# The last head set of an attention block as two halves, the last MLP by token tile, and a shared PV bank

## The chip, the cores and the metric

The kernel runs on one core of a Trainium2 chip. The metric is the device time of one execution in microseconds (us). Engines are named as in the profile: PE is TensorE, ACT is ScalarE, DVE is VectorE, POOL is GpSimd, SP is SyncE, which issues most DMAs.

## The reference

A transformer block with conditioning (adaLN) over 2048 tokens of width 640, with 32 heads of width 20 and an MLP of width 1536 whose gate and up parts are multiplied without a nonlinearity:

```python
mod = (_silu(c) @ w_mod).reshape(1, 6, 1, -1)          # sa, ca, ga, sb, cb, gb
h = _layernorm(x) * (1 + ca) + sa
x = x + ga * attention(h, wqkv, wo)                    # softmax(q k^T / sqrt(20)) v, 32 heads, then wo
h = _layernorm(x) * (1 + cb) + sb
x = x + gb * (((h @ w_gate) * (h @ w_up)) @ w_down)
```

Inputs and output are bfloat16.

## The kernel before

The program is written by a planner that runs in the kernel's own Python. Every operation becomes a `Task` with an engine, a duration, dependencies, a priority, and buffer slots; `Sched.run` steps through planned time, and on each engine starts the ready task of lowest priority number. PE has its own chooser, `pick_pe`. `emit_program` then writes each engine's list in that order, with semaphore waits only where a dependency crosses engines. So one changed duration, slot or setting moves instructions all over the program.

**Attention.** The queries are cut into five chunks, `CHUNKS`: three of 512 tokens, two of 256. The heads go in 8 sets of 4. A chunk and a set are an *item* (40 items). An item consists of *units*: 512 columns of scores of one head (keys by queries), made on PE at L1480 from `QT` and `KT`, four heads in four row groups of 32. Two units fill two PSUM banks, and one exponential on ACT (L1517, `PP<-ps_all` 128x1024) turns them into probabilities. Some units go to DVE instead, four to a *quad*, as `QUADS` says by chunk and set: L1541 turns each score bank into an integer (task P1, tile `DB`), L1573 and L1581 make two terms of 2048 columns (`DSS`), and a product of the two is done by DVE in one piece (L1578) or by POOL in four (L1593). Quads count as two terms in the next step, so a unit on DVE costs PE two products where one on ACT costs one.

**PV.** At L2038 the probabilities are multiplied by `Vf` (V with a column of ones), four heads in four column groups, and summed over all keys of the item in one PSUM bank, number 7 (`BPV`). At an item's end a DVE transpose (L1665, T1) empties the bank; the next item's first PV product waits for it (`st_pv["free"]`). Then come a reciprocal (L1669), a product on POOL (L1671), a transpose back (L1679), and small DMAs on SP (L1692) that place the head outputs in `Ocp`.

**PSUM.** Banks 0, 1, 3 and 4 hold the scores for ACT. A pool `G` of banks 5, 6 and 2 serves P1 units and every other product; bank 7 is PV's.

**Other work on PE** fills the time between scores, in `Round`s that each take one bank of `G`, run a chain of products and end with an evacuation: the projections K, Q and V, and for each finished chunk the suffix (`suffix`): the output projection with residual (L1763), layer norm, transposes (L1796), gate and up (`gsb` takes the gate out of PSUM, L1865 or L1896 multiplies it into `hprod`), down, and the residual sum (L1919) that a DMA writes out (L1928). Most of these products use 32-column tiles (L939), the last chunk's full 128-column ones (L935). K and Q of head set 0 (and of some others) come straight out of PSUM; the rest is packed in blocks of 128 rows (L1199) and goes through DRAM (`k_rows`, `q_rows`) to be laid out by head. V is made per 128 tokens in the parts that `V_PARTS` lists:

```python
V_PARTS = [[0, 4], [4, 8]]
K_ALL = (0,)
LATEQ = (3,)
```

`K_ALL` names the 512-token chunks whose K is made directly for all sets, `LATEQ` those whose Q is made only in the second attention chunk. The suffix of chunk c runs between the scores of chunk c+1. The last chunk's has no scores beside it; its DMAs, with weights from `stx` and `stg`, are issued earlier. Its output projections need the last head set's result only in their last product (`wo7`, `OcT`), which is split off (`OP_EARLY`).

**Filler.** Two fillers keep PE active where it has nothing ready: `do_fill` (L2403, L2405) with products of the identity, and `zero_fill` (L2377), which adds products of a zero tile `zt` to the PV bank. `STAGE` holds the chooser's settings item by item (thresholds for PV bursts, for filling, for holding PE free for a score).

Of the kernel before, what the change touches and what calls it, by code (L numbers as in the profile page):

```python
# [12 lines left out]
SEM = 60.0  # L13
# [21 lines left out]
class Task:  # L35
    __slots__ = ("head", "hval", "hknow", "eng", "dur", "lat", "deps", "emits", "ctr", "prio", "gate", "acq", "on_start", "slots",
                 "start", "done", "needed", "val", "know", "nleft", "ready", "users", "name", "mode", "seq", "rt", "sem",
                 "nbytes", "cond", "alt", "land", "lk")

    def __init__(self, eng, dur, emits, deps=(), ctr=None, prio=0.0, lat=None, gate=0, acq=(), on_start=None,  # L40
# [26 lines left out]
        self.lk = 0  # L67
        if lat is None:
            lat = {"pe": PE_DRAIN, "act": ACT_LAT, "dve": DVE_LAT, "pool": 60.0}.get(eng, 0.0)
        self.lat = lat  # L70

# [49 lines left out]
class Sched:  # L121
# [32 lines left out]
    def locked(self, eng, task):  # L154
        if not task.lk:
            return False
        if self.lk_end["pool" if eng == "dve" else "dve"] > self.t:
            return True
        if task.lk == 2:
            tt = max(self.t, self.free_at["dve"])  # L160
            for d in sorted(self.readyl["dve"], key=lambda x: (x.prio, x.seq)):
# [89 lines left out]
    def pull(self, eng):  # L251
        p = self.pend[eng]
        while p and p[0][0] <= self.t:
            _, _, task = heapq.heappop(p)
            self.readyl[eng].append(task)

    def step_engine(self, eng):
# [4 lines left out]
        rl.sort(key=lambda x: (x.prio, x.seq))  # L262
        for k, task in enumerate(rl):
            if task.gate > self.progress or (task.cond is not None and not task.cond()):
# [13 lines left out]
    def steal(self):  # L278
# [4 lines left out]
        for task in self.readyl["dve"]:  # L283
            if task.alt is not None and (best is None or (task.prio, task.seq) < (best.prio, best.seq)):
                best = task
        if best is None or self.free_at["dve"] <= self.t and best is min(self.readyl["dve"], key=lambda x: (x.prio, x.seq)):
# [41 lines left out]
def emit_program(nc, sched, nsem_dma=56):  # L328
# [97 lines left out]
    with nc.Block() as block:  # L426
# [20 lines left out]
        def _(e):  # L447
# [5 lines left out]
QUADS = ((0, 4, 3, 3, 3, 4, 4, 4),  # L453
# [35 lines left out]
K_ALL = (0,)  # L489
# [6 lines left out]
V_PARTS = [[0, 4], [4, 8]]  # L496
# [14 lines left out]
FILL_Z, Z_LATE = 3300.0, 0.0  # L511
# [9 lines left out]
OPFIRST = 0  # L521
# [4 lines left out]
LATEQ = (3,)  # L526
LATEQ_A = 2
LATEQ_F = 0.534
# [4 lines left out]
    0: {"X_LATE": -179.96, "D_RES": 74, "EAGER": 9, "PVMAX": 14, "HOLD": 95, "PVTOL": 249, "D_LATE": 16, "PVMIN": 2, "PVCAP": 12, "FILL_MIN": 4190.746, "TPRIO": 0.75, "XDPRIO": 1.343, "XBACK": 0, "STEAL_GAP": 200, "FILL_Z": 3300.0, "Z_LATE": 0.0},  # L533
    1: {"HOLD": 91, "D_LATE": 10, "PVMAX": 7, "Z_LATE": 89.79, "FILL_MIN": 4705.4},
    2: {"DL": 0.376, "D_LATE": 17, "D_RES": 29, "FILL_Z": 3209.68, "EAGER": 9, "FILL_MIN": 4297.75},
    3: {"STEAL_GAP": 200, "PVMAX": 5, "FILL_MIN": 4667.05, "PVTOL": 199},
    4: {"XBACK": 0, "PVMAX": 9, "EAGER": 4},
    5: {"EAGER": 7, "D_RES": 27, "PVCAP": 8, "XBACK": 2, "FILL_MIN": 3800.69, "PVMIN": 5, "PVTOL": 124, "HOLD": 155},
    6: {"PVCAP": 12, "FILL_MIN": 4293.4, "D_LATE": 12, "PVMIN": 2, "EAGER": 8, "TPRIO": 0.87},
    7: {"DL": 0.501, "PVCAP": 8, "PVTOL": 347, "FILL_MIN": 4921.03, "D_LATE": 18, "HOLD": 155, "PVMAX": 9},  # L540
    8: {"PVCAP": 15, "PVMAX": 3, "FILL_MIN": 3871.81, "Z_LATE": -44.68, "FILL_Z": 3323.21},
    9: {"X_LATE": -14.35, "PVCAP": 14, "FILL_Z": 3486.74, "XBACK": 0, "HOLD": 80, "PVMIN": 5, "D_LATE": 12, "PVMAX": 5},
    10: {"PVMAX": 8, "X_LATE": -27.967, "EAGER": 8, "D_LATE": 15, "PVCAP": 14, "XBACK": 0, "HOLD": 155, "FILL_Z": 3693.44, "Z_LATE": -95.95},
    11: {"DL": 0.443, "X_LATE": 44.62, "FILL_MIN": 4364.854, "PVTOL": 245, "HOLD": 134, "PVMAX": 9, "PVCAP": 13},
    12: {"DL": 0.459, "FILL_MIN": 5309.94, "D_LATE": 7, "STEAL_GAP": 194.93, "X_LATE": -138.337},
    13: {"DL": 0.417, "D_RES": 4, "HOLD": 84, "PVMAX": 6, "TPRIO": 0.787, "PVMIN": 5, "STEAL_GAP": 145.61, "PVCAP": 13, "XBACK": 3, "FILL_MIN": 4476.6, "FILL_Z": 2814.04},
    14: {"D_LATE": 14, "D_RES": 22, "FILL_MIN": 4216.3, "EAGER": 10, "X_LATE": 83.38, "STEAL_GAP": 200, "PVTOL": 324, "FILL_Z": 3248.09},
    15: {"X_LATE": -197.47, "FILL_MIN": 4338.164, "EAGER": 13, "Z_LATE": -100, "D_RES": 5, "HOLD": 95, "PVCAP": 15},
    16: {"FILL_MIN": 4469.77, "D_RES": 61, "HOLD": 88, "PVCAP": 11, "PVMIN": 3, "PVTOL": 299, "STEAL_GAP": 121.93, "EAGER": 10},
    17: {"D_LATE": 17, "PVMAX": 10, "PVMIN": 5, "STEAL_GAP": 195.663, "FILL_MIN": 4059.54},  # L550
    18: {"FILL_MIN": 5006.36, "D_RES": 10, "X_LATE": 47.914, "FILL_Z": 3093.15, "HOLD": 65, "Z_LATE": -17.94, "PVTOL": 174},
    19: {"DL": 0.471, "D_LATE": 18, "FILL_MIN": 3976.707, "X_LATE": -139.98, "HOLD": 110},
    20: {"DL": 0.391, "D_LATE": 14, "PVCAP": 16, "FILL_MIN": 5166.07, "FILL_Z": 3745.27, "HOLD": 125, "STEAL_GAP": 143.97},
    21: {"D_RES": 10, "PVCAP": 20, "HOLD": 111, "PVMAX": 6, "PVMIN": 2, "D_LATE": 19, "X_LATE": -18.564, "STEAL_GAP": 193.54, "FILL_MIN": 4920.22},
    22: {"PVMAX": 6, "FILL_MIN": 3112.0, "D_RES": 17, "X_LATE": -139.27, "EAGER": 6, "D_LATE": 16, "PVCAP": 10, "FILL_Z": 2965.54, "PVTOL": 224},
    23: {"PVTOL": 197, "PVMAX": 8, "D_RES": 20, "Z_LATE": -56.49, "STEAL_GAP": 273.34, "FILL_MIN": 5000.65, "EAGER": 4, "HOLD": 170},
    24: {"DL": 0.464, "PVCAP": 13, "PVMAX": 9, "PVMIN": 2, "FILL_MIN": 3616.91, "EAGER": 7, "STEAL_GAP": 200, "X_LATE": 41.65, "HOLD": 125, "XDPRIO": 0.3, "D_LATE": 14},
    25: {"DL": 0.549, "STEAL_GAP": 200, "HOLD": 129, "X_LATE": 33.41, "D_RES": 10, "FILL_MIN": 3705.17, "PVCAP": 13, "D_LATE": 18, "PVMIN": 5, "Z_LATE": 116.92, "PVMAX": 9, "XBACK": 1},
    26: {"DL": 0.411, "D_RES": 15, "X_LATE": -208.68, "PVMAX": 9, "PVCAP": 14, "STEAL_GAP": 200, "FILL_MIN": 3859.63, "XBACK": 3, "EAGER": 8},
    27: {"DL": 0.473, "D_LATE": 6, "PVMAX": 6, "EAGER": 2, "D_RES": 75, "PVTOL": 249, "PVMIN": 2, "X_LATE": -47.659, "FILL_MIN": 4666.31},  # L560
    28: {"PVCAP": 13, "X_LATE": 63.33},
    29: {"PVCAP": 14, "PVMAX": 7, "D_RES": 46, "FILL_MIN": 3820.529, "HOLD": 65, "PVTOL": 299},
    30: {"X_LATE": -28.91, "PVCAP": 18, "FILL_MIN": 3782.61, "D_LATE": 16, "EAGER": 6, "PVMAX": 4, "STEAL_GAP": 217.05, "PVTOL": 224},
    31: {"D_RES": 19, "FILL_MIN": 4905.173, "D_LATE": 15, "PVMIN": 2, "X_LATE": 36.868, "HOLD": 125, "PVTOL": 274},
    32: {"PVMIN": 1, "D_LATE": 17, "D_RES": 78, "XDPRIO": 0.559, "XBACK": 0, "X_LATE": 56.51, "FILL_Z": 2800.13, "EAGER": 3},
    33: {"DL": 0.442, "STEAL_GAP": 199.702, "D_LATE": 18, "PVCAP": 15, "PVMAX": 4, "PVTOL": 353, "D_RES": 11, "PVMIN": 2, "HOLD": 100, "XDPRIO": 1.634, "EAGER": 4, "Z_LATE": 171.35, "FILL_MIN": 5185.17},
    34: {"X_LATE": 150, "D_LATE": 22, "HOLD": 117, "FILL_MIN": 3598.58, "EAGER": 5},
    35: {"PVMIN": 5, "PVMAX": 8, "FILL_MIN": 2725.18, "STEAL_GAP": 179.748, "X_LATE": -77.47, "HOLD": 121, "D_LATE": 8},
    36: {"DL": 0.524, "PVMIN": 2, "D_RES": 10, "X_LATE": -6.364, "FILL_MIN": 4268.89, "PVMAX": 8, "HOLD": 33},
    37: {"D_LATE": 12, "PVTOL": 179, "PVCAP": 13, "FILL_MIN": 5500, "X_LATE": -66.154, "TPRIO": 0.3, "XBACK": 0, "XDPRIO": 1.88, "HOLD": 65},  # L570
    38: {"D_RES": 60, "PVMAX": 7, "PVTOL": 450, "HOLD": 67, "D_LATE": 16},
    39: {"FILL_MIN": 3000, "D_LATE": 13, "PVTOL": 258, "X_LATE": -31.59, "PVCAP": 16, "PVMAX": 5, "EAGER": 8, "HOLD": 140, "XBACK": 3},
# [15 lines left out]
def build_kernel(nc, A_x, A_wqkv, A_wo, B_x, B_w_gate, B_w_up, B_w_down, c, w_mod, out):  # L588
# [62 lines left out]
    zt = alloc("zt", [128, 32], BF16)  # L651
# [33 lines left out]
    Vf = alloc("Vf", [128, NT * H * VW], BF16)  # L685
# [56 lines left out]
    set_r = (hprod, h2T, xck, xn2)  # L742
    ntail = CHUNKS[-2][1]
# [20 lines left out]
    G = Slots([5, 6, 2] if HEADG else [5, 6], "G")  # L764
# [3 lines left out]
    BPV = 7  # L768
# [113 lines left out]
    p_zt = pool(100, lambda e: e.memset(zt[:], 0.0), prio=5) if FILL_Z > 0.0 else None  # L882
# [1598 lines left out]
```

## Time and profile before

| | us |
|---|---|
| median of 3 runs | 811.79 |
| the runs | 813.02, 810.24, 811.79 |
| profiled execution: span from first to last instruction | 809.0 |
| PE busy | 792.6 |
| ACT busy | 763.8 |
| DVE busy | 703.1 |
| POOL busy | 321.2 |

The profiled execution has no other time than its span; the median lies 2.8 us above it. A busy share is an average over a start, in which projections feed the first scores, a long middle, and an end without scores, so the stages have to be read one by one. The granted clock of PE is 1.00. In a timeline, a row gives the start, how long the merged group lasts, the engine, the line, the operation, how many, and in brackets the idle time before it with what ended it. In a windows row the columns are the window, its length, the busy time and number of instructions, the granted clock, the DMA share and GB/s.

### The profile page before, as it was taken

What the parts mean: (1) busy time and instruction counts of PE and PEld (TensorE: products, weight loads), DVE (VectorE), ACT (ScalarE), POOL (GpSimd) and SP (SyncE); (2) the same over time, 40 slices, a digit from 0 to 9 for tenths busy, and PEclk for the clock granted to TensorE, in tenths of its full rate; (3) what the DMA queues carried; (4) which work ended last, traced back from release to release, by engine and by line L of the source; (5) the groups of instructions that cost most, each with busy time, mean ns of one, the idle gap of its engine ahead of it and who ended that gap; (6) DMA issues with size and microseconds to landing.
All of it is one profiled execution on the core that took longest, in us unless ns stands there. A gap on an engine that the chain in (4) does not pass through costs nothing.

```text
span 809.0 us, 29314 instructions
## 1 busy us (share of the span) xinstructions
PE 792.6 (98%) x12585; PEld 303.1 (37%) x12585; DVE 703.1 (87%) x1273; ACT 763.8 (94%) x853; POOL 321.2 (40%) x330
## 2 busy tenths in 40 slices
PE   9999999999999999999999999999999999999998
PEld 4433333222232333233233232343244433444567
DVE  7979987999999999999998999999699875778973
ACT  7899999999999999999999999999999999999912
POOL 3304244565524442164335334444265340443520
PEclk9999999999999999999999999999999999999999
DMA  9633211113330144100301221001201236005520
GB/s 306 210 87 105 71 46 42 47 36 123 91 67 25 40 112 132 26 9 20 85 25 31 48 57 30 11 22 53 56 6 31 55 78 144 23 30 125 115 70 17
DMA packets 116447, 54.74 MB, mean 68 GB/s; under 512 B 83915, under 2 KB 116319, under 8 KB 116319
## 3 DMA queue, kind: packets, MB, share of 16 engines
q1 hardware_dynamic: 115391, 51.72, 24.3%
q8 instruction: 100, 1.64, 0.8%
q10 hardware_dynamic: 928, 1.15, 0.4%
q14 instruction: 28, 0.23, 0.1%
HBM read 41.85 MB, written 8.41 MB: 62 GB/s over the span
## 4 chain that ended last, share of the span: by engine, by line
PE 52%; ACT 34%; DVE 8%; issue 4%; SPq 1%; DMA 0%; POOL 0%; ACTq 0%; POOLq 0%
ACT PP L1517 34%; PE ps_all L1480 17%; PE ps_all L939 15%; PE ps_all L2038 11%; DVE DB L1541 3%; PE ps_all L935 3%; PE ps_all L1199 3%; PE ps_all L1135 1%; PE ps_all L2403 1%; DVE DSS L1581 1%; DVE DSS L1578 1%; PE ps_all L2405 1%; DVE DSS L1573 1%; PE ps_all L1096 1%; DVE wd L1463 0%
## 5 line engine op out<-in xcount | busy, mean ns | idle before, releaser
L1517 ACT ACTIVATE PP<-ps_all 128x1024 bf16<-128x1024 f32 x808 | 743.9, 1144 | 5.2 <-PE ps_all L1480 4.4
L1593 POOL TENSOR_TENSOR DSS<-DB,DSS 128x512 bf16<-128x512 bf16 x224 | 254.9, 1156 | 324.6 <-DVE DSS L1581 236.0
L1541 DVE TENSOR_SCALAR DB<-ps_all 128x512 int16<-128x512 f32 x432 | 288.5, 684 | 45.0 <-PE ps_all L1480 42.2
L1480 PE MATMUL ps_all<-QT,KT 32*128 32x512 bf16 (+1 forms) x2560 | 315.7, 340 | 8.3 <-ACT PP L1517 5.9
L1480 PEld LDWEIGHTS ps_all<-QT,KT 32*128 32x128 bf16 x2560 | 82.4, 91 | 266.3 <-ACT PP L1517 230.0
L2038 PE MATMUL ps_all<-PP,Vf 128*32 128x512 bf16 (+1 forms) x2032 | 158.8, 343 | 0.3 <-DVE OT L1665 0.3
L939 PE MATMUL ps_all<-h2T,stg 128*32 128x512 bf16 (+1 forms) x1744 | 118.1, 345 | 1.2 <-DVE DB L1541 0.9
L2038 PE MATMUL ps_all<-DSS,Vf 128*32 128x512 bf16 (+2 forms) x1056 | 84.4, 343 | 0.4 <-POOL DSS L1593 0.2
L1573 DVE TENSOR_SCALAR DSS<-DB 128x2048 int16<-128x2048 int16 x108 | 75.5, 699 | 0.5
L1581 DVE TENSOR_SCALAR DSS<-DB 128x2048 int16<-128x2048 int16 x108 | 75.8, 702 | 0.0
L2038 PEld LDWEIGHTS ps_all<-PP,Vf 128*32 128x32 bf16 x2032 | 44.6, 94 | 78.4 <-issue 72.1
L1671 POOL TENSOR_TENSOR OTn<-OT,invT 128x512 bf16<-128x512 f32 (+1 forms) x39 | 37.8, 970 | 89.4 <-DVE invT L1669 89.3
L1578 DVE TENSOR_TENSOR DSS<-DB,DSS 128x2048 bf16<-128x2048 bf16 x52 | 67.1, 1290 | 0.2
L939 PE MATMUL ps_all<-wd,hprod 128*32 128x320 bf16 (+1 forms) x1348 | 60.1, 282 | 0.0
L939 PEld LDWEIGHTS ps_all<-h2T,stg 128*32 128x32 bf16 x1744 | 37.2, 95 | 35.7 <-issue 23.6
L939 PEld LDWEIGHTS ps_all<-wd,hprod 128*32 128x32 bf16 x1348 | 29.7, 96 | 19.7 <-issue 11.3
L2038 PEld LDWEIGHTS ps_all<-DSS,Vf 128*32 128x32 bf16 (+1 forms) x1056 | 26.4, 95 | 19.7 <-issue 8.2
L939 PE MATMUL ps_all<-wV,hT 128*32 128x320 bf16 (+1 forms) x692 | 31.7, 291 | 0.0
L1885 DVE CAST gsb<-ps_all 128x512 bf16<-128x512 f32 x36 | 24.5, 680 | 8.1 <-PE ps_all L939 8.0
L1199 PE MATMUL ps_all<-hT,wq 128*32 128x512 bf16 x375 | 31.5, 382 | 0.0
L1665 DVE STREAM_TRANSPOSE OT<-ps_all 128x512 f32<-128x512 f32 (+1 forms) x40 | 24.1, 603 | 7.3 <-PE ps_all L2038 7.3
L939 PE MATMUL ps_all<-wo,Ocp 128*32 128x320 bf16 (+1 forms) x648 | 29.8, 283 | 0.6 <-DVE DB L1541 0.2
(124 smaller groups left out, 531.6 us busy)
## 6 DMA issues: line engine op xcount, KB each, us to landing
stg<-in_B_w_gate_dram SPq DMA_DIRECT2D x50, 160.0 KB
stg<-in_B_w_up_dram SPq DMA_DIRECT2D x50, 160.0 KB
QT<-q_rows SPq DMA_DIRECT2D x22, 128.0 KB
KT<-k_rows SPq DMA_DIRECT2D x84, 32.0 KB
wm<-in_w_mod_dram SPq DMA_DIRECT2D x3, 800.0 KB
x<-in_A_x_dram SPq DMA_DIRECT2D x7, 320.0 KB
xck<-in_A_x_dram SPq DMA_DIRECT2D x3, 640.0 KB
wd<-in_B_w_down_dram SPq DMA_DIRECT2D x1, 1920.0 KB
```

Of the source, the lines that this page charges most:

```text
L939: return lambda e, b: e.matmul(ps[32 * x:32 * x + 32, b, c0 + o:c0 + o + w], lhs()[:, 32 * x:32 * x + 32], rhs() if w == n else rhs()[:, o ...
L1199: f = [lambda e, b_, k=k, x=x: e.matmul(ps[x:x + min(32, w - x), b_, :], wx[:, k, r0 + x:r0 + min(x + 32, w)], hT[tc][:, k, :], tile_posit ...
L1480: ems.append(lambda e, i=i, kt=kt: e.matmul(dstf()[:, i * u.n:(i + 1) * u.n], KT[32 * u.s:32 * u.s + 32, u.j, kt * 128:(kt + 1) * 128], QT ...
L1517: return e.activation(PPs[g % 2][:, cellp["p"], 0:nu * 512], ps[:, b0:b0 + nu, :].rearrange("p b c -> p (b c)"), AFT.Exp, scale=ESCALE)
L1541: return e.tensor_scalar(DBl[st_["slot"]][:, x * 512:(x + 1) * 512], bank(cell["b"]), EBIAS, 0.0, op0=ALU.add, op1=ALU.max)
L1573: return e.tensor_scalar(DSl[st_["ss"][0]][:, :], DBl[st_["slot"]][:, :], 0x7F, 0x3F00, op0=ALU.bitwise_and, op1=ALU.bitwise_or)
L1578: return e.tensor_tensor(d, DBl[st_["slot"]][:, :].bitcast(BF16), d, ALU.mult)
L1581: return e.tensor_scalar(DSl[st_["ss"][1]][:, :], DBl[st_["slot"]][:, :], 0x7F80, 2, op0=ALU.bitwise_and, op1=ALU.bitwise_or)
L1593: return e.tensor_tensor(d, DBl[st_["slot"]][:, x * w:x * w + w].bitcast(BF16), d, ALU.mult)
L1671: f3 = lambda e: e.tensor_tensor(OTn[:, 0:n].rearrange("p (b c r) -> p b r c", c=32, r=2), OT[:, 0:n].rearrange("p (b r c) -> p b r c", c= ...
L1885: f = lambda e: e.tensor_copy(gsb[:, gs, 0:n], ps[:, r.b["b"], 0:n])
L2038: ems.append(lambda e, i=i, kt=kt, stt=stt, stp=stp: e.matmul(ps[32 * s:32 * s + mc, BPV, 0:u.n], Vf[:, (kt * H + 4 * u.j + s) * VW:(kt * ...
```

## The change

- The last item (chunk 4, set 7) becomes two items of 128 queries each (`SPLITJ`, `spans`), without quads (`QHALF`), where the whole item had two. A unit still has 512 score columns, now four key tiles by 128 queries.
- The suffix of the last chunk is done per tile of 128 tokens: transposes and their evacuation per tile (`t_h2t`), gate and up in rounds of two 128-wide blocks of the MLP for one tile (`hp_t`), output projections per tile as soon as that tile's head outputs are there; only the second tile's last products are split off.
- PV takes a bank from `G`, which has now 5, 6, 2 and 7, at an item's first product, and gives it back at T1. Two items may be open at once (`PV_OPEN`), the second one only if two banks are free (`PV_KEEP`). `zero_fill` goes.
- V is made in four parts, K of chunk 0 is packed for all sets but the first, and the Q of a second 512-token chunk is made late.
- Chunk 1 has a residual buffer of its own, `xckb`, in the place of dead queries.
- Output projections of every chunk get an earlier priority (`OPFIRST`), the settings in `STAGE` are others, and a few changes make the planner itself run faster (sorted ready lists, `dead` tasks).

```diff
-V_PARTS = [[0, 4], [4, 8]]
+V_PARTS = [[0, 2], [2, 4], [4, 6], [6, 8]]
-K_ALL = (0,)
+K_ALL = ()
-OPFIRST = 0
+OPFIRST = 1500
-LATEQ = (3,)
-LATEQ_A = 2
-LATEQ_F = 0.534
+LATEQ = (2, 3)
+LATEQ_A = -20
+LATEQ_F = 0.35
+SPLITJ = 1
+QHALF = ((0, 0), (0, 0))
+PV_W4 = 430.0
+PV_OPEN = 2
+PV_KEEP = 2
...
-    G = Slots([5, 6, 2] if HEADG else [5, 6], "G")
+    G = Slots([5, 6, 2, 7], "G")
-    BPV = 7
...
+    if SPLITJ:
+        del items[-SPLITJ:], spans[-SPLITJ:], nqs[-SPLITJ:]
+        for hf in range(2):
+            for x in range(SPLITJ):
+                items.append((NC - 1, NSET - SPLITJ + x))
+                spans.append((128 * hf, 128))
+                nqs.append(QHALF[hf][x])
...
+    xckb = at("xckb", [128, 4, D], BF16, qt_off)
+        if ci % 2 and not alt:
+            xck = xckb
+            xfree = outs_r[1] + sfx_done["qd0"] + x0_done
...
         def one(u, srcf, deps, name):
+            info = item_info[u.item]
+            if info["bank"] is None:
+                info["bank"], rel = G.take(G.avail()[1], 1)
+                deps = deps + rel
...
+            for tl in range(ntl):
+                for f2 in range(0, FT, 2):
+                    mms = []
+                    for w_ in range(2):
+                        for x in range(2):
+                            cell = gu_w[f2 + x][0][w_]
+                            for k in range(KD):
+                                f = full(128, lambda k=k, cell=cell: cell["t"][:, k, :],
+                                         lambda k=k, tl=tl: h2T[:, k, tl * 128:(tl + 1) * 128], k == 0, k == KD - 1,
+                                         256 * w_ + 128 * x)
+                                mms.append((C128, f))
...
-        return FILL_Z > 0.0 and sc.recent(t) < FILL_Z and zero_fill(t)
+        return t > FILL_T0 and fill_ok(t, fill_deps) and do_fill(t)
```

More of the change, by code (lines that the diff above doesn't have):

```diff
@@ L282, in steal @@
         best = None
-        for task in self.readyl["dve"]:
-            if task.alt is not None and (best is None or (task.prio, task.seq) < (best.prio, best.seq)):
+        rd = [x for x in self.readyl["dve"] if not x.dead]
+        for task in rd:
+            if task.alt is not None:
                 best = task
-        if best is None or self.free_at["dve"] <= self.t and best is min(self.readyl["dve"], key=lambda x: (x.prio, x.seq)):
+                break
+        if best is None or self.free_at["dve"] <= self.t and best is rd[0]:
             return False
@@ L1660, in item_end_tasks @@
             z_tail[ci] = [pool(1200, lambda e: e.memset(Ocp[:, ci % 2, KD - 1, :], 0.0), list(oc_free[ci - 2]), prio=9)]
[L1661 removed]
+        qo, n = spans[it]
+        half = ci == NC - 1 and n < CHUNKS[ci][1]
         nb32 = n // 32
@@ L1674, in item_end_tasks @@
             invT[:, 0:nb32].rearrange("p (b r) -> p b r", r=2).unsqueeze(3).to_broadcast([128, nb32 // 2, 2, 32]), ALU.mult)
-        if T3_POOL and it < len(items) - 1:
+        direct = j == NSET - 1 and ci == NC - 1
+        if T3_POOL and not direct:
             t3 = pool(n * 2.2 + 200, f3, [t2], prio=0)
@@ L1742, in suffix @@
         d_xc = dma("sp", 128 * ntl * D * 2, lambda e: e.dma_start(xck[:, 0:ntl, :], xv[:, t0:t0 + ntl, :]),
-                   (first if alt else bd.get("out", []) + v_last), prio=15, gate=max(0, gb + XC_G))
+                   (first if alt else xfree), prio=15, gate=max(0, gb + XC_G))
         t_xn2 = []
@@ L1848, in suffix @@
             gs = fc % 2
+            if tail and SPLITJ:
+                gu_w.append((wbuf, dm, use_x))
+                continue
             if n <= 256 and GU_ONE:
@@ L1933, in suffix @@
         bd["tr"] = tr_l[-1:]
-        bd["out"] = outs
+        if not alt:
+            outs_r[ci % 2] = outs
     t1s = {}
@@ L2027, in pv_balance, with vdeps @@
         return res + dd
+    def vdeps(u):
+        d = [v_ready[(kt, vp[u.j])] for kt in u.kts]
+        if u.j == NSET - 1 and u.s == 3:
+            d += [v_ready[(kt + 1, 0)] if kt < NT - 1 else p_vz for kt in u.kts]
+        return d
     def pv_emit(u, srcf):
@@ L2031, in pv_emit @@
         ems = []
-        mc = VW if (4 * u.j + s) % 16 == 15 else 32
+        mc = VW if s == 3 and u.j + 1 in [b for _, b in V_PARTS[:-1]] else 32
+        bk = item_info[it]["bank"]
         for i, kt in enumerate(u.kts):
@@ L2053, in pv_issue, with one @@
     def pv_issue(cands, t):
-        it = st_pv["item"]
-        info = item_info[it]
         start = mode_start("P", t)
         colt = [0.0] * 4
-        w = PV_W * clk()
-        last = None
+        last = {}
+        def one(u, srcf, deps, name):
+            info = item_info[u.item]
+            if info["bank"] is None:
+                info["bank"], rel = G.take(G.avail()[1], 1)
+                deps = deps + rel
+            task = Task("pe", 216.0, pv_emit(u, srcf), deps + vdeps(u), ctr="pep", mode="P", name=f"{name}{u.item}")
+            w = (PV_W4 if u.n < 256 else PV_W) * clk()
+            b = max(colt[u.s], max(colt) - w)
+            task.seq = 0
+            sc.left += 1
+            sc.finish_issue(task, start + b, w)
+            colt[u.s] = b + w
+            sc.activity(start + b, 128.0)
+            last[u.item] = task
+            return task
         for kind, x in cands:
@@ L2103, in pv_issue @@
         sc.free_at["pe"] = sc.pe_end
-        if info["left"] == 0:
-            t1 = t1s[it]
-            t1.deps = [last]
-            sc.left -= 1
-            sc.add(t1)
-            st_pv["free"] = [t1]
+        for it in sorted(last):
+            if item_info[it]["left"] == 0:
+                t1 = t1s[it]
+                t1.deps = [last[it]]
+                sc.left -= 1
+                sc.add(t1)
+        while st_pv["item"] < len(items) and item_info[st_pv["item"]]["left"] == 0:
             st_pv["item"] += 1
@@ L2329, in pick_pe @@
         if cands:
-            info = item_info[it]
             ring_low = ring() < RINGLOW
-            ending = info["left"] <= len(cands)
+            ending = item_info[it]["left"] <= sum(1 for k, x in cands if (x.item if k == "a" else d_state[x[0]]["item"]) == it)
             force = ring_low or ending
```

343 lines of the change are left out of this document (184 added, 159 removed), and 4 rows, old and new, of the table QUADS.

## The prediction

> **What bounds the kernel now.** I began with the page: which engine is busy, and with what.
>
> ```profile
> PE 792.6 (98%) x12585; PEld 303.1 (37%) x12585; DVE 703.1 (87%) x1273; ACT 763.8 (94%) x853; POOL 321.2 (40%) x330
> L1517 ACT ACTIVATE PP<-ps_all 128x1024 bf16<-128x1024 f32 x808 | 743.9, 1144 | 5.2 <-PE ps_all L1480 4.4
> ```
>
> PE is called 98% busy, but its ends are modelled, so this alone does not make it the bound. ACT spends 743.9 of its 763.8 us on 808 exponentials (L1517). Next come the windows of that line alone:
>
> ```profile
> 400.00:500.00 100.00, 100.00 (x110) 1.00 0.18 43
> 500.00:600.00 100.00, 100.00 (x110) 1.00 0.11 30
> ```
>
> 110 exponentials per 100 us is 0.909 us each, with no gap: here ACT sets the pace (the 1.144 us of the page overlap). The timeline of ACT at the start shows where it does not:
>
> ```profile
> 16.13 7.40 ACT L1517 ACTIVATE PP<-ps_all 128x1024 bf16<-128x1024 f32 x8
> ...
> 27.07 7.44 ACT L1517 ACTIVATE PP<-ps_all 128x1024 bf16<-128x1024 f32 x8 [0.16 <-PE ps_all L1480]
> 35.80 7.48 ACT L1517 ACTIVATE PP<-ps_all 128x1024 bf16<-128x1024 f32 x8 [1.29 <-PE ps_all L1480]
> ...
> 44.62 11.30 ACT L1517 ACTIVATE PP<-ps_all 128x1024 bf16<-128x1024 f32 x12 [0.32 <-PE ps_all L1480]
> ...
> 57.22 2.85 ACT L1517 ACTIVATE PP<-ps_all 128x1024 bf16<-128x1024 f32 x3 [0.75 <-PE ps_all L2038]
> 60.93 17.54 ACT L1517 ACTIVATE PP<-ps_all 128x1024 bf16<-128x1024 f32 x19 [0.85 <-PE ps_all L1480]
> 78.86 16.61 ACT L1517 ACTIVATE PP<-ps_all 128x1024 bf16<-128x1024 f32 x18 [0.39 <-PE ps_all L1480]
> ```
>
> 58 exponentials start before 78.86, which at 0.909 from 16.13 would take 52.7 us; they take 62.7. So 10.0 us are lost at the head, in six gaps: 3.7, 1.5, 1.5, 1.7, 1.0 and 0.7 us. The timeline of PE in the first gap says why:
>
> ```profile
> 23.43 1.25 PE L1135 MATMUL ps_all<-hT,wq 128*32 128x512 bf16 x20
> 24.51 1.25 PE L1135 MATMUL ps_all<-hT,wk 128*32 128x512 bf16 x20
> 25.59 1.12 PE L939 MATMUL ps_all<-wV,hT 128*32 128x320 bf16 x28
> 26.64 0.40 PE L1480 MATMUL ps_all<-QT,KT 32*128 32x512 bf16 x4
> ```
>
> PE works without a break from 22.41 to 26.64 on projections; the scores wait behind them. A stretch of 4.2 us makes ACT 3.7 late, one of 2.1 (33.31 to 35.37) makes it 1.5 late: lateness is the stretch less about 0.55. The last exponential ends at 770.19, and the tail that follows belongs to PE:
>
> ```profile
> 769.57 2.26 PE L939 MATMUL ps_all<-h2Tt,stg 128*32 128x256 bf16 x76
> ...
> 772.57 0.84 PE L939 MATMUL ps_all<-h2Tt,stg 128*32 128x256 bf16 x24 [0.52 <-DMA stg<-in_B_w_up_dram]
> ...
> 775.35 2.08 PE L935 MATMUL ps_all<-wo,Ocp 128*128 128x320 bf16 x14 [0.39 <-DMA Ocp<-OcT]
> ...
> 783.53 0.73 PE L1796 MATMUL ps_all<-ident,xn2c 128*128 128x128 bf16 x10
> 784.19 2.22 PE L939 MATMUL ps_all<-wd,hprodt 128*32 128x320 bf16 x60
> 786.34 11.09 PE L935 MATMUL ps_all<-h2Tc,stx 128*128 128x256 bf16 x100
> 797.27 2.35 PE L935 MATMUL ps_all<-h2Tc,stg 128*128 128x256 bf16 x20
> 799.45 6.71 PE L935 MATMUL ps_all<-wd,hprodc 128*128 128x320 bf16 x60
> ```
>
> The chain that ended last is PE from 775.35 on. The span is thus 16.1 (first exponential) + 808 x 0.909 = 734.5 + 10.0 (head) + 9.6 (later handoffs) + 38.8 (tail) = 809.0 us. The median of the runs, 811.79, lies 2.8 above it; I carry that over.
>
> **More exponentials.** The last head set had two quads on DVE, its two halves have none. Eight units of 512 columns go back to ACT: 812 instead of 808, 4 x 0.909 = **+3.6 us**, on the path. Eight P1 (684 ns) and their terms leave DVE, which costs or saves nothing there.
>
> **Head.** Nothing ahead of the first exponential changes in amount. In the changed kernel's order of instructions, V comes in 160-column products, so fewer V columns are due early, K of chunk 0 is packed, and Q of rows 1024 to 1535 moves into the second chunk. Behind the eighth exponential PE now has 40 K products (2 x 1.08 us by the rows above), 40 V products of 160 columns (half of the 320-column 0.136 per four: 0.7) and 4 PV (0.23): about 3.2 us, so 2.7 late instead of 3.7. The second stretch becomes longer: 40 K, 20 V, 4 transposes, 4 PV, 3.1 us, so 2.5 late instead of 1.5. The other long ones shrink from 2.1 and 1.8 to four of 0.9 to 1.1 us; stretches of that length cost between 0 and 0.7 before, I take 0.3 each, 1.2. Together 6.4 instead of 10.0: **-3.6 us**, bounds -4.5 and -2.0 (0.7 each). The K rows that now go through DRAM (28 more loads, 0.43 us of SP each) are due at the 33rd exponential, near 50 us; issued after 25, they take the 9 us that the first packed block took from 30.7 to its last load at 39.4. V's casts grow from 32 to 64; a 320-column one takes 484 ns, so between 242 and 484 each, at most 15 us, hidden on DVE, which loses 12 products of 1290 ns to POOL.
>
> **Middle.** The PV bank now comes out of the common four banks at an item's first product, so the next item need not wait for the transpose L1665. PE's waits on it sum to 0.5 us in the trace: nearly nothing to win. Adding up PE's work between scores by row durations, the excess over 0.53 us (0.909 less a 0.22 score and 0.16 of mode changes) after the 80th score group falls from 9.3 to 8.0 us. Scaled on the 9.6 us of handoffs: **-1.4 us**, bounds -4.8 (half of them gone) and +3, since a new order meets other waits. The zero filler that is removed has no row in the page's trace; the other filler falls from 316 to 180 products, in time when PE had nothing else. The 40 products more on POOL (1156 ns each, 46 us) leave it at 45%. The second residual buffer frees L1742 of its 4.5 us wait on output DMAs, on SP, with nothing late behind it.
>
> **Tail.** One might expect that half of the last MLP now runs under the exponentials. The order says otherwise: all 240 gate and up products, all 192 down products of the chunk before and all 60 of the last stand behind the last scores, as before. What changes: 7 of 24 output projections run ahead of the last exponential's products, -0.95; 16 of the last PV products do too, and are half as wide, -0.6; three waits (0.52, 0.39, 0.17) lose their cause, -1.1: no DVE terms feed the last items, item 38's DMAs are issued 16 exponentials earlier. All 120 leftover gate/up products now follow, where 22 had run: +0.7. DVE, with a 6.7 us queue ahead of the second tile's transposes, adds +0.3. Then 240 products of 128 columns replace 120 of 256 (13.1 us from 786.34 to 799.45). The nearest row is the transposes at 783.53: the same shape, each with its own 128x128 weights, (0.73 - 0.22)/9 = 0.057 us apart; 240 x 0.057 = 13.6, +0.5. Sum **-1.2 us**, bounds -2.6 and, with weight loads in series (below), +9.
>
> [...]
>
> **Sum.** +3.6 - 3.6 - 1.4 - 1.2 = -2.6: span 806.4, median 809.2.
>
> **Rivals.** *The order does better than its sums* (0.22): the head reaches -4.5, the handoffs -4.8, the tail -2.6: with +3.6 that is -8.3 at best, 803.5; half way from the forecast, 806. For it: shorter stretches nearly everywhere. Against: most handoffs are under 0.2 us, which order cannot remove.
>
> *Banks run short* (0.13, the slower side): at each of 40 item borders two PV banks can be open at once, leaving two banks for P1 units and projections, where three were. The trace has PE waiting on DB L1541 twice, 1.1 us in all, with three. At 0.25 us per border, half of such a wait, it costs 10 us: 819. It decides from 0.13 us per border (5 us: my 2.6 and the bound below). Against: no projection was pushed out into the tail.
>
> *Weight loads bound the last MLP* (0.05): loads of 128x128 take about 0.096 us; if they don't overlap each other, 240 x (0.096 - 0.057) = +9.4, 818.6. For it: in 790 to 800 us PEld is busy 8.87 of 10 us with 92 loads, half as many as to come. Against: the transposes, and the 25 one-column products of L960 in 0.77 us, which load as much each and start 0.025 apart. [...]
>
> *The clock falls without the filler* (0.05): the first five or so filler products at L2403 start 0.43 us apart, later ones 0.22, so a slow state exists; a stretch of 8 us at half speed would cost about 8: 817. Against: the granted clock is 1.00 in every window.
>
> That the halves do not move work out of the tail is no rival, but my reading of the order.
>
> **How the numbers follow.** The forecast holds 0.55, its own range 807 to 812. The measurement tells about 0.3%, 2.4 us: faster means under 809.35, which halves the forecast's case: 0.28 and 0.27. Faster: 0.28 + 0.22 = 0.50; same 0.27; slower 0.13 + 0.05 + 0.05 = 0.23. The range 804 to 816 leaves out the bank case, half of the weight-load case and the best end of the better one, together 0.2.
>
> **What would show it.** 812 exponentials, the first at 16.1; the gap behind the eighth near 2.7 us, behind the sixteenth 2.5, none over 0.7 later; the last exponential's end near 769; tail 37 to 38 us; the 240 products 0.057 apart. Wrong, if the products stand 0.08 or more apart, if PE rows wait on L1555 or T1 at the borders, if the granted clock leaves 1.00, or if 412 to 770 us hold fewer than 109 exponentials per 100 us.

## The result, and the profile after

The changed kernel took 815.83 us (median of four runs, 814.20 to 818.07) beside 811.47 of the kernel before in the same session (810.24 to 813.02). The ratio is 1.0056, 95% interval 1.0035 to 1.0077: slower by about 4.5 us, where 809.2 was forecast. The profiled execution has a span of 813.5 us, and its own time is 815.35. From the page:

```profile
PE 790.4 (97%) x13447; PEld 318.1 (39%) x13447; DVE 687.6 (85%) x1295; ACT 765.4 (94%) x849; POOL 365.4 (45%) x370
L1531 ACT ACTIVATE PP<-ps_all 128x1024 bf16<-128x1024 f32 x812 | 749.3, 1113 | 6.8 <-PE ps_all L1494 4.9
```

There are 812 exponentials (now L1531), and in the middle they still set the pace, 110 per 100 us:

```profile
400.00:500.00 100.00, 100.00 (x110) 1.00 0.16 37
```

The timeline of ACT shows the head, and something that was not there before:

```profile
26.43 7.44 ACT L1531 ACTIVATE PP<-ps_all 128x1024 bf16<-128x1024 f32 x8 [0.23 <-PE ps_all L1494]
...
36.48 17.71 ACT L1531 ACTIVATE PP<-ps_all 128x1024 bf16<-128x1024 f32 x19 [0.68 <-PE ps_all L1494]
54.53 21.19 ACT L1531 ACTIVATE PP<-ps_all 128x1024 bf16<-128x1024 f32 x23 [0.34 <-PE ps_all L1494]
75.98 12.19 ACT L1531 ACTIVATE PP<-ps_all 128x1024 bf16<-128x1024 f32 x13 [0.27 <-PE ps_all L1494]
90.04 1.02 ACT L1531 ACTIVATE PP<-ps_all 128x1024 bf16<-128x1024 f32 x1 [1.87 <-PE ps_all L1494]
91.70 1.02 ACT L1531 ACTIVATE PP<-ps_all 128x1024 bf16<-128x1024 f32 x1 [0.64 <-PE ps_all L1494]
93.57 3.98 ACT L1531 ACTIVATE PP<-ps_all 128x1024 bf16<-128x1024 f32 x4 [0.85 <-PE ps_all L2154]
```

The head has two large gaps instead of six. At 90 us there are three new ones. Taking the start-to-start time of each exponential less its undisturbed pitch of 0.905 (0.9047 in the sums) as its lateness, exponentials 71 to 73 (counted from 0, as the program names its rows) are late by 2.07, 0.76 and 0.97 us. In the timeline of PE the first one is an idle stretch ahead of a score row:

```profile
87.12 0.38 PE L2154 MATMUL ps_all<-PP,Vf 128*32 128x512 bf16 x2
89.61 0.39 PE L1494 MATMUL ps_all<-QT,KT 32*128 32x512 bf16 x3 [2.11 <-issue]
```

The row holds two units for ACT and one for DVE, which belongs to a later head set. "issue" means that the profile names no releaser; in the program this row waits for the load of that set's Q. The timeline of SP shows this load as one of the two of L1272 at 85.69:

```profile
77.91 4.24 SPq L1263 DMA_DIRECT2D KT<-k_rows  x8
82.19 1.73 SPq L1250 DMA_DIRECT2D q_rows<-KPA  x3
...
85.69 1.31 SPq L1272 DMA_DIRECT2D QT<-q_rows  x2
```

DVE had emptied the bank with the packed Q block by 79.10 us (L1216). Its stores (L1250) stood on SP behind eight KT loads of about 0.53 us each and were issued from 82.19. In the program the load waits for them to land; it was issued 1.77 us after the last of them had been. In the kernel before, the timeline of SP has the same load later:

```profile
88.33 0.89 SPq L1267 DMA_DIRECT2D QT<-q_rows  x2
```

There the first row that reads it (S73) starts at 92.01, with no idle time ahead of it. In the changed kernel PE is free for the row that reads it first (S71) at 87.50. So the load comes 2.6 us earlier than before, and its user 4.5. After the idle stretch the granted clock of PE falls from 1.00 to 0.52 and 0.63 (windows of PE: window, length, busy, granted clock, DMA share, GB/s):

```profile
88.00:90.00 2.00, 0.39 (x7) 1.00 0.24 69
90.00:92.00 2.00, 2.00 (x51) 0.52 0.06 16
92.00:94.00 2.00, 2.00 (x32) 0.63 0.00 0
```

That makes exponentials 72 and 73 late too. In the tail, the products in question:

```profile
791.54 4.92 PE L940 MATMUL ps_all<-h2Tc,stx 128*128 128x128 bf16 x85
...
804.11 6.71 PE L940 MATMUL ps_all<-wd,hprodc 128*128 128x320 bf16 x60
```

From 791.54 to 804.11 stand 225 of the 240 products of 128 columns: 12.57 / 225 = 0.056 us apart. From the start of the last exponential to the end the tail takes 38.3 us, before 39.8.

The balance of the two profiled spans, 813.5 against 809.0: first exponential +0.2, four exponentials +3.6, lateness of the first 58 from 10.2 to 7.2, -3.0, exponentials 71 to 73 +3.8, all the others behind the 58th +1.5 (14.2 against 12.7), tail -1.6. That is all of the 4.5.

### The profile page after: what moved, and what is told of

Read it like the earlier page. It is cut to its first block, busy times and chain, and to the rows that moved or that the text cites. A ratio compares the mean times of both kernels' runs of the same rounds, so it can differ in the third digit from the quotient of the medians.

```text
span 813.5 us, 31169 instructions
## 1 busy us (share of the span) xinstructions
PE 790.4 (97%) x13447; PEld 318.1 (39%) x13447; DVE 687.6 (85%) x1295; ACT 765.4 (94%) x849; POOL 365.4 (45%) x370
## 4 chain that ended last, share of the span: by engine, by line
ACT 44%; PE 42%; issue 6%; DVE 5%; DMA 1%; SPq 0%; ACTq 0%; DVEq 0%
ACT PP L1531 44%; PE ps_all L1494 14%; PE ps_all L944 13%; PE ps_all L2154 9%; PE ps_all L940 3%; DVE DB L1555 2%; PE ps_all L1204 1%; DMA wm<-in_w_mod_dram 1%; PE ps_all L1140 1%; PE ps_all L1101 1%; PE ps_all L2487 1%; DVE DSS L1595 0%; DVE wd L1477 0%; DVE DSS L1592 0%; DVE DSS L1587 0%
## 5 line engine op out<-in xcount | busy, mean ns | idle before, releaser
L1531 ACT ACTIVATE PP<-ps_all 128x1024 bf16<-128x1024 f32 x812 | 749.3, 1113 | 6.8 <-PE ps_all L1494 4.9
L1607 POOL TENSOR_TENSOR DSS<-DB,DSS 128x512 bf16<-128x512 bf16 x264 | 301.3, 1161 | 327.9 <-DVE DSS L1595 254.2
L1494 PE MATMUL ps_all<-QT,KT 32*128 32x512 bf16 (+2 forms) x2624 | 319.9, 336 | 13.2 <-ACT PP L1531 5.6
L1555 DVE TENSOR_SCALAR DB<-ps_all 128x512 int16<-128x512 f32 x424 | 282.5, 683 | 54.8 <-PE ps_all L1494 52.5
L2154 PE MATMUL ps_all<-PP,Vf 128*32 128x512 bf16 (+2 forms) x2112 | 162.8, 338 | 0.0
L2154 PE MATMUL ps_all<-DSS,Vf 128*32 128x512 bf16 (+3 forms) x1024 | 84.9, 347 | 0.2
L2154 PEld LDWEIGHTS ps_all<-PP,Vf 128*32 128x32 bf16 (+1 forms) x2112 | 46.5, 94 | 83.4 <-issue 77.0
L1592 DVE TENSOR_TENSOR DSS<-DB,DSS 128x2048 bf16<-128x2048 bf16 x40 | 51.5, 1288 | 0.1
L944 PE MATMUL ps_all<-wV,hT 128*32 128x160 bf16 x1280 | 38.2, 238 | 0.9 <-issue 0.5
L1204 PE MATMUL ps_all<-hT,wk 128*32 128x512 bf16 (+1 forms) x360 | 31.6, 382 | 0.1
L1686 DVE STREAM_TRANSPOSE OT<-ps_all 128x512 f32<-128x512 f32 (+2 forms) x41 | 24.3, 592 | 7.9 <-PE ps_all L2154 7.8
L1959 DVE TENSOR_TENSOR hprod<-ps_all,gsb 128x512 bf16<-128x512 f32 x36 | 24.5, 681 | 7.6 <-PE ps_all L944 7.4
```

Of the source, the lines that this page charges most:

```text
L944: return lambda e, b: e.matmul(ps[32 * x:32 * x + 32, b, c0 + o:c0 + o + w], lhs()[:, 32 * x:32 * x + 32], rhs() if w == n else rhs()[:, o ...
L1204: f = [lambda e, b_, k=k, x=x: e.matmul(ps[x:x + min(32, w - x), b_, :], wx[:, k, r0 + x:r0 + min(x + 32, w)], hT[tc][:, k, :], tile_posit ...
L1494: ems.append(lambda e, i=i, kt=kt: e.matmul(dstf()[:, i * u.n:(i + 1) * u.n], KT[32 * u.s:32 * u.s + 32, u.j, kt * 128:(kt + 1) * 128], QT ...
L1531: return e.activation(PPs[g % 2][:, cellp["p"], 0:nu * 512], ps[:, b0:b0 + nu, :].rearrange("p b c -> p (b c)"), AFT.Exp, scale=ESCALE)
L1555: return e.tensor_scalar(DBl[st_["slot"]][:, x * 512:(x + 1) * 512], bank(cell["b"]), EBIAS, 0.0, op0=ALU.add, op1=ALU.max)
L1592: return e.tensor_tensor(d, DBl[st_["slot"]][:, :].bitcast(BF16), d, ALU.mult)
```

## Experiments

All times are medians; each ratio is to the kernel before, run on the same chip beside it.

**The Q load earlier (e1).** Only SP's list is changed, after planning:

```diff
+    later, stores, ql = sp[83:90], sp[90:93], sp[95]   # 7 KT loads, 3 q_rows stores, the QT load
+    # new order: stores, later[:3], ql, later[3:]
```

> Only SP's order differs from the changed kernel: at 78 us the three q_rows stores of the last packed Q block, and the QT load of its head set, stand ahead of seven KT loads that nobody needs before 90 us; the orders of PE, ACT, DVE and POOL are the same. Theory (the late Q block): PE no longer sits idle for 2.1 us at 87.5, the granted clock stays 1.00 between 88 and 96 us, exponentials 71 to 73 lose their lateness of 2.07 + 0.76 + 0.97, and the time falls by 3.5 to 4.6 us, to 811 to 812. Rival (four more exponentials and the new order of the middle cost the time, and a stall at 88 us only moves lateness that would come later): the stall goes, but the span falls by less than 1.5 us, to 814 or more.

Measured: 812.12 us, ratio 1.0021 (1.0008 to 1.0034), span 809.4. The stores are issued from 79.00, the load at 82.41. The granted clock is 1.00 in all windows of the profiled execution, and the 13 exponentials from 77.72 run through:

```profile
77.72 12.16 ACT L1531 ACTIVATE PP<-ps_all 128x1024 bf16<-128x1024 f32 x13
90.18 10.74 ACT L1531 ACTIVATE PP<-ps_all 128x1024 bf16<-128x1024 f32 x11 [0.30 <-PE ps_all L2154]
```

The span falls by 4.1, the ratio by 0.35 points, 2.8 us. The theory holds: with the order of PE, ACT, DVE and POOL untouched, the late Q block is worth about 3 to 4 of the 4.5 us. The lateness doesn't come back later: behind exponential 150 it is 12.0 us here and 11.8 before.

**Filler in the wait (e2).** Ten products of the identity ahead of the waiting row:

```diff
+    row = next(t for t in pe if t.name == "S71")
+    # 10 x matmul(ps[:, 3 or 4, :], ident, ident), inserted in front of row
```

> The changed kernel with ten products of the identity (128x512, 0.22 us each) on PE just ahead of the score row that waits for the late Q load, into the score banks that this row then overwrites; the load stays as late. Theory: exponential 71 stays about 2.1 us late, since the load sets it, but PE is active in the wait, so that the granted clock stays near 1.00 after 90 us and exponentials 72 and 73 lose their 0.76 + 0.97: the time falls by about 1.7 us, to 814. Rival (the clock has nothing to do with the idle time, and 72 and 73 are late because PE catches up with its V products): they stay late and the time is the same within 0.3 us, or longer if the filler delays the row.

Measured: 814.27 us, ratio 1.0049 (1.0033 to 1.0064). Exponential 71 is 2.16 late, 72 and 73 are not, and the clock is 1.00 from 90 to 96 us:

```profile
93.46 4.95 ACT L1531 ACTIVATE PP<-ps_all 128x1024 bf16<-128x1024 f32 x5 [1.96 <-PE ps_all L1494]
```

So of the 3.8 us of the stall about 2.1 are the wait, and 1.7 the clock that falls behind it. This split rests on the profile: the ratio falls by only 0.07 points, 0.6 us, and its interval overlaps that of the changed kernel. The execution that was profiled, 817.53, had another fall, 0.50 from 22 to 28 us, behind 0.86 us of idle time of PE between 18 and 22 us; it made the gap behind the eighth exponential 4.9 us.

**The last item whole (e3), and quads in its halves (e4).** Both share the changed kernel's order up to 749 us:

```diff
-SPLITJ = 1
+SPLITJ = 0
```

> The changed kernel with the last item left whole (SPLITJ = 0: 256 queries, two quads on DVE, 808 exponentials, the last MLP by 256 columns); the order of all engines is the same up to 749 us. Theory (the prediction's terms): four exponentials fewer, -3.6, and the old tail back, +1.2 to +1.6: 813.5 to 814 where the changed kernel has 815.8. Rival (the split is worth what its quads cost, or more): 815.8 or longer, with a tail behind the last exponential longer by 3.6 us or more than the 38.3 of the changed kernel.

```diff
-QHALF = ((0, 0), (0, 0))
+QHALF = ((1, 0), (1, 0))
```

> The changed kernel with one quad in each half of the last head set (QHALF = ((1, 0), (1, 0)): 808 exponentials); the order is the same up to 749 us. Theory: four exponentials fewer, -3.6 on ACT, and DVE's terms for the last items come late and give 1 to 2 us back in the tail: 813.5 to 814. Rival (DVE's terms bound the tail): the tail grows by 3.6 us or more, and the time is 815.8 or longer.

Measured: 814.96 us (ratio 1.0053, 1.0037 to 1.0068) and 815.38 us (1.0056, 1.0043 to 1.0069), against 1.0056 of the changed kernel. Both have 808 exponentials, and both tails are longer, 42.1 and 42.3 us, by 3.8 and 4.0. So the rivals hold: with the settings of this order the four exponentials are given back in the tail. With quads in the halves PE stands there for DVE:

```profile
783.39 1.13 PE L944 MATMUL ps_all<-wd,hprodt 128*32 128x320 bf16 x28 [1.04 <-DVE hprodt L1928]
```

It waits another 0.6 us for a term from POOL, and in e3 0.9 us for `hprodt` and 0.9 for a DVE term; the changed kernel's tail has no such wait. That is less than half of what the tails grow by; the rest was not taken apart.

In three of e3's six runs the mean granted clock is 1.000 (813.2 to 813.8 us), in the other three it is 0.996 or 0.998 (816.1 to 817.2), although the order at 88 us is the changed kernel's in all of them. So the clock does not fall behind that idle stretch every time.

**V in two parts (e6); K of chunk 0 directly (e7).** These are planned anew with settings not made for them, so only exponentials 1 to 150 are read, and not the whole times (824.67 and 824.86 us).

```diff
-V_PARTS = [[0, 2], [2, 4], [4, 6], [6, 8]]
+V_PARTS = [[0, 4], [4, 8]]
```

> The changed kernel with V in two parts as before (V_PARTS = [[0, 4], [4, 8]]); the planner orders all anew with settings that were not made for it, so only the first 150 exponentials are read. Theory (V in four parts makes the gain at the head, by putting fewer V columns ahead of the scores, and it also moves the Q block of exponential 71 early): the first 58 exponentials are late by about 10 us again (7.2 in the changed kernel, 10.3 before), and there is no stall of 2 us between exponentials 60 and 100. Rival (K of chunk 0 through DRAM makes the gain and the stall): 7.2 us at the head as in the changed kernel, and the stall stays.

```diff
-K_ALL = ()
+K_ALL = (0,)
```

> The changed kernel with K of chunk 0 made directly for all sets as before (K_ALL = (0,)), again read only up to exponential 150. Theory (SP's backlog comes from the 28 more KT loads, V's parts only shift the work on PE): the head stays at about 7.2 us, SP issues 28 loads fewer, and no score row between exponentials 60 and 100 waits over 0.5 us for a Q load. Rival (the backlog is not what makes the Q load late): the head is the same and a stall of 1 to 2 us stays between 60 and 100.

Lateness of the first 58 exponentials: 9.4 with V in two parts, 7.9 with K made directly (7.2 in the changed kernel, 10.2 before). So most of the gain at the head, 2.2 us, hangs on V's four parts. On the stall the first theory was wrong. With V in two parts it is there again, 2.55 us, behind sixteen KT loads that end at 88.79, with the Q load at 92.52 (timelines of SP and PE):

```profile
79.81 8.98 SPq L1263 DMA_DIRECT2D KT<-k_rows  x16
...
92.52 3.13 SPq L1272 DMA_DIRECT2D QT<-q_rows  x2
```

```profile
97.38 0.40 PE L1494 MATMUL ps_all<-QT,KT 32*128 32x512 bf16 x4 [2.55 <-issue]
```

With K made directly SP issues 84 KT loads instead of 112, and no row between exponentials 60 and 100 waits for a Q load; the largest lateness there, 0.82, follows PV products. Its timeline of SP has the Q load at

```profile
82.98 0.83 SPq L1272 DMA_DIRECT2D QT<-q_rows  x2
```

So in these orders the stall goes with K through DRAM. But e7 changes two things at once: the load comes 2.7 us earlier than in the changed kernel, and in the program's order its first user is row S82 instead of S71. With the 3.9 us from issue to use that the changed kernel shows, the load would have been usable at 86.9, ahead of the 87.5 at which PE was free for S71; that is an estimate.

**One open PV bank (e8).**

```diff
-PV_OPEN = 2
+PV_OPEN = 1
```

> The changed kernel with only one item allowed to hold a PV bank (PV_OPEN = 1), as with the fixed bank before, but out of the same four banks; ordered anew. Theory (the prediction's: waits for the PV bank at item borders were worth nearly nothing): the exponentials behind number 150 are late by about 12 us in all, as in the changed kernel (12.5) and before (11.8), and PE waits for the transpose that empties the bank for less than 1 us in sum. Rival (the second open item carries the borders of this order): 16 us or more, with waits on the transpose at a good part of the 40 borders.

One run (822.09 us), planned anew. Behind exponential 150 the lateness is 14.1 us, against 12.5 in the changed kernel and 11.8 before, between the two expectations. PE waits for the transpose that empties the bank (tile OT) once, 0.2 us. It shows no large price of the borders either way. The late Q load is here too, and the profile names it ("DMA QT<-q_rows", 1.8 us).

**Idle spots and the clock (e5, e9; e11 and e12 are the kernels of e1 and e9 once more).** Of the 12 runs with the early Q load, 7 have a mean clock of 1.000 and take 811.3 to 812.2 us; 5 lie below it, at 812.6 to 816.1 (the mean granted clock over the whole execution). Of 51 runs of the kernel before beside these experiments, 2 lie below 1.000. Two attempts to remove idle spots, on top of the early Q load:

```diff
+    # V2.0's first product 7 times more, PV0's first product 2 times more
```

> The kernel with the early Q load (e1), and PE kept active in its two idle spots of the head (0.50 us at 17.0, 0.29 us at 19.1): the first product of the third V round is made eight times instead of once (160 columns, some 0.07 us each), the first PV product three times (0.22 us each); each repeat starts its sum anew, so the result is the same. Theory (idle PE in the head lets the clock fall): of e1's 12 runs the seven at a mean clock of 1.000 took 811.3 to 812.2, the five below it 812.6 to 816.1; in the profile of e2 the clock was 0.50 from 22 to 28 us, behind idle spots at 19 us. With the spots filled all runs have a mean clock of 1.000 and the median is 811.3 to 811.8, without runs above 812.5. Rival (the clock falls by chance, or for a later idle spot): three to six of some ten runs stay below 1.000, the median stays near 812.1 or rises by the 0.3 us that the repeats may cost.

```diff
+    # 18 score rows made twice: S3, S40, S156, S172, S227, S291, ... S788
```

> The kernel with the early Q load (e1), and 18 score rows made twice, each the row that stands ahead of an idle spot of PE of more than 0.25 us in e1's profile (20 such spots ahead of 770 us, 6.7 us in sum; before has 9, 4.6 us). A repeat takes 0.2 to 0.3 us of the idle time and starts its sums anew. Theory (short idle spots let the granted clock fall by chance, and each fall costs 1 to 4 us): fewer runs below a mean clock of 1.000 than e1's 5 in 12, at most 2 in 10, and a median of 811.3 to 811.8. Rival (the falls have nothing to do with these spots): 4 or more in 10 again and a median of 812 or more; a repeat that delays its exponential costs up to 0.2 us each, 3.6 in all, which would show as lateness in the profile.

Measured: 814.31 us with 4 of 7 runs below 1.000, and 812.93 us with 3 of 11, whose other runs lie at 812.1 to 813.0. So neither attempt removed the falls. By the ratios (1.0038 and 1.0027 against 1.0021) they cost 1.4 and 0.5 us; the intervals overlap. And 3 of 11 runs are too few to tell from 5 of 12. The first one failed for a reason that the profile shows. In its timeline the idle spot at 17 us is still there (first row), and the second row is the changed kernel's:

```profile
17.33 0.92 PE L944 MATMUL ps_all<-wV,hT 128*32 128x160 bf16 x41 [0.31 <-issue]
```

```profile
17.66 0.44 PE L944 MATMUL ps_all<-wV,hT 128*32 128x160 bf16 x13 [0.50 <-issue]
```

It stands behind the 221st matmul record of PE in both, though other products stand there. This points at a place in the instruction stream and not at a wait for data; no run shows the cause. Each of the two kernels was profiled once more, for where the falls come:

> The kernel with the early Q load (e1) once more, for a profile of an execution in which the granted clock falls; 5 of its 12 runs had a mean clock below 1.000. Theory (the fall comes in the head, behind the idle spots between 16 and 20 us, as in the profile of e2): if the mean clock is below 1.000, the windows between 20 and 30 us show 0.5 to 0.9 and the gap behind the eighth exponential is over 4 us instead of 2.5. Rival (falls come anywhere, wherever 3 to 4 us hold some 0.8 us of idle time): a window behind 100 us shows it, and the head is as in e1.

> The kernel with 18 score rows made twice (e9) once more, for the same reason; 3 of its 11 runs had a mean clock below 1.000. Theory (the head): its head is that of e1 but for one repeat at 18 us, so a fall shows again between 20 and 30 us. Rival: a window behind 100 us shows it.

The first (815.45 us) caught one, at neither of the expected places; the second (812.82) none. It came ahead of the first exponential, behind 1.71 us in which PE waited for the modulation weights (`wm`). That exponential is 3.1 us late; 2.0 of it were there at the first product with these weights (9.83, against 7.83 in e1's profile), so about 1.1 came behind it:

```profile
8.00:10.00 2.00, 0.29 (x8) 1.00 1.12 321
10.00:12.00 2.00, 2.00 (x47) 0.69 1.10 348
12.00:14.00 2.00, 2.00 (x30) 0.50 0.87 264
```

Three profiles thus have a fall in the head: e11's at 11 us, e2's at 21, and e8's at 22. The idle spot at 17 us, longer than 0.15 us in nine of the twelve profiles with V in four parts, is missing in just these three. So it is not what these falls need. What they share is that PE had waited for something that hangs on an input load: for `wm` in e11, and for normalised tokens (`xn`, at 20.1 us) in e2 and e8, 0.52 and 0.77 us, a wait on `xn` at that place that the other profiles don't show. Waits for `wm` without a fall behind them occur too (1.25 us in the changed kernel's profile, 1.21 in e7's). That late inputs cause the falls is a guess that no run tests.

**A better kernel (e10).** The early Q load, the whole last item, and the chooser's settings of items 36 to 41 searched anew for it:

```diff
-SPLITJ = 1
+SPLITJ = 0
+    q_first(sc)        # the early Q load
-    36: {"DL": 0.524, "D_RES": 0, "X_LATE": -94.5, "PVMIN": 1, "X_HALF": 76.4},
+    36: {"DL": 0.524, "D_RES": 72, "X_LATE": -147.188, "PVMIN": 2, "X_HALF": -27.821, ...},
...
```

> A candidate for a better kernel: the changed one with the early Q load, the last item left whole (SPLITJ = 0, two quads, 808 exponentials), and chooser settings of items 36 to 41 searched anew for it; up to 700 us the order is that of e1. Theory (the exponentials are worth their 0.905 us each when the tail does not grow): 808 exponentials, -3.6 against e1, and a tail of 39 to 41 us instead of 38.3, +0.7 to +2.7: a span of 806.5 to 808.5, 808.4 to 810.4 as a time, faster than before's 810.7 to 811.3. Rival (the tail gives back what the quads save, as in the kernel with a quad in each half): a tail over 41.5 us, and no gain against e1.

Measured: 809.76 us (809.22 to 811.69 in 11 runs) against 811.04, ratio 0.9986 (0.9976 to 0.9996), span 807.9. It has 808 exponentials, and the tail takes 38.8 us. So the theory holds: it beats the kernel before by about 1.1 us (0.3 to 1.9) and, by the two ratios, the changed one by 5.7. The last MLP runs there with 256 columns again:

```profile
785.39 11.09 PE L943 MATMUL ps_all<-h2Tc,stx 128*128 128x256 bf16 x100
```

## Why the prediction was wrong

**More exponentials, +3.6: right as a term, wrong as a loss by itself.** 812 came, at 0.905. But the two kernels with 808 show that with this order's settings the quads' saving comes back in the tail. It need not: with settings searched for it, e10 has 808 and a tail of 38.8 us, and lies 2.8 us below e1 by the ratios. So the prediction could not price the exponentials without the tail.

**Head, -3.6: -3.0.** The gap behind the eighth exponential is 2.5 (2.7 forecast), behind the sixteenth 2.8 (2.5), and the later ones are 0.5 and 0.6. The mechanism was right; by e6 and e7, 2.2 us of it hang on V's four parts and 0.7 on K.

**Middle, -1.4: +5.3. This is the step that failed.** 3.8 of it is the stall, and that goes back to a sentence of the head: the 28 more KT loads were set against the 33rd exponential, at which the first K rows are due, and found to have slack. They do. But the sum stopped at the loads themselves and did not name what stands behind them on SP. The Q stores and the Q load of a unit that needs them in row S71 were moved from "nobody waits" (in the kernel before, 88.33 for the load and 92.01 for its row) to "a score row waits". The load was issued earlier than before; its user came earlier still. The price of the whole was put at nothing, and PE stood idle for 2.11 us. The list of what would show the forecast wrong named P1 units, T1 and the clock, and not a DMA; its last sign, fewer than 109 exponentials per 100 us from 412 to 770 us, could tell nothing, since both kernels have 108.4 there. The other part is the scaling of PE's work between scores onto the handoffs: it gave -1.4, and with the Q load early the middle is still 1.4 us worse than before (1.2 of it between exponentials 58 and 150; what makes these 1.4 us stays open: the late Q of rows 1024 to 1535, the earlier output projections, `xckb` and the settings were not tried one by one). Its base was mis-sized too. A count of 110 in 100 us is rounded up: the pitch is 0.905, not 0.909, so 12.7 us and not 9.6 lay in the later handoffs. And the change between scores and other products takes 0.10 us each way in the rows, 0.2 in all (in the changed kernel's rows, scores of 0.22 us start at 18.03, V products of 0.07 at 18.35, the next scores at 18.53), where 0.16, a figure that no row shows, was put in. The upper bound of +3 had no row behind it.

**Tail, -1.2: -1.6.** The products stand 0.056 us apart, 0.057 forecast; the other terms of the tail were not taken apart.

**The rivals.** Banks did not run short: PE's waits on DB L1555 are 2.9 us in sum, 1.1 more than before, not 10 (before they are 1.8 in four rows; the prediction read one of them, 1.1). Its waits on T1 grow from 0.5 to 0.9. Weight loads did not bound the last MLP: its products stand 0.056 us apart, and one load of theirs takes 0.098 (median). That the range took in half of that case was the author's estimate; no run shows a spacing between the two. The clock (0.05) was nearer than its chance said: it fell, not for lack of filler in general (e1, which lacks the zero filler too, shows 1.00 in every window), but behind idle stretches of PE (2.11 us in the changed kernel's profile, 1.71 in e11's); 1.7 us of the stall, and more in some runs. (Thirteen filler products stand 0.43 us apart at the start of that trace, not five.) That the range held the time was luck: its upper end, 816, stood for banks that run short and for weight loads in series, and neither came.

What stays open: why the granted clock falls in more runs than before (15 of 43 runs of the four kernels with the early Q load). The kernel before has 2 of 51. Three profiles caught a fall in the head, at 11, 21 and 22 us. That the idle spots cause the frequency was argued, and the attempts to fill them did not show it.

## What to carry to other kernels

When a change adds transfers to an in-order queue, don't stop at whether the new ones are in time: list every transfer that now stands behind them, and for each the first instruction that waits for it and what else that instruction holds up. Here three stores were issued 3.1 us after their data was ready, behind eight loads. A DVE unit bundled into one score row with two ACT units made ACT wait for a load that it did not need. And price an idle stretch of PE at more than its length, since the granted clock may fall behind it: here it cost 1.7 us on top of 2.1.

## What the runs showed of the hardware

- How long a fall of the granted clock lasted, estimated from the windows of 2 us with 0.50, the lowest clock that one of them shows, as the clock in a fall: (1 - clock) x 2 us / 0.5, summed, gives 3.4 us at 90 us in the changed kernel, 3.4 in the profile with the fall at 11 us (e11), and 6.8 at 21 us with the filler (e2). In the changed kernel it came behind 2.11 us in which PE stood idle; the same order at 88 us went with a mean clock of 1.000 in three of e3's six runs. What decides whether a fall follows is not shown.
- The first filler products stand 0.43 us apart and later ones 0.22. The step between the two comes at 7.3 us in the kernel before and at 4.7 in the changed one. The eleven filler products from 3.88 us on take 4.24 and 2.95 us there, 2.85 in e7 and 4.42 in e2; worked out from these lengths, the step lies between 4.6 and 7.7 us, an estimate. What sets it is not shown.
- PE stood still for 0.2 to 0.5 us behind its 221st matmul in nine of the twelve profiles with V in four parts, also where another product stood there (e5). The two kernels whose V products have 320 columns (before and e6) show no such gap: PE is busy for 2.00 of the 2 us from 16 on.
- A KT load of 32 KB took SP 0.42 us to issue in the median of the changed kernel, with single ones from 0.30 to 1.70; the eight ahead of the stores took 4.24 together. The Q load of 128 KB was used 3.9 us after its issue, at 89.61.
